# Half-height matmuls in pairs, sums on GpSimd and a written-out TensorE order in a block of attention and squared-ReLU FFN

## The chip, the cores and the metric

The kernel runs on one core of a Trainium2 chip. The metric is device time in microseconds (us) of one execution, as the median of several runs. TensorE (PE in the profile, its weight loads PEld) multiplies; VectorE (DVE), ScalarE (ACT) and GpSimd (POOL) do elementwise work; SyncE (SP) issues the transfers (DMA). Matmul results go to PSUM, a small memory that GpSimd has no part in here; all else lies in SBUF.

## The reference

One sequence of 2048 tokens with 576 features, all in float32:

```python
xn = _layernorm(x, axis=-1)
return x + _A_ref(xn, A_wqkv, A_wo) + _B_ref(xn, B_w1, B_b1, B_w2, B_b2)
# A: q, k, v = xn @ wqkv, 32 heads of 18; each token attends to 8 earlier
#    tokens at distances 0, 2, ... 14; then @ wo
# B: h = xn @ w1 + b1 (4608 wide); r = max(h, 0); (r * r) @ w2 + b2
```

## The kernel before, in words

**Number format.** Every float32 operand of a matmul is split into a high part in a shorter format that TensorE reads (float32r) and a low part, the rest. A product is then three matmuls, high by high, high by low and low by high. Feature chunks are 128 rows; 576 is four chunks and 64 rows. The last 64 features stand twice in a chunk of their own: for the activations (`xe`) the high part fills 64 rows and the low part the other 64, so one matmul with the high half of W1 covers two of the three terms, and one with the low half covers the third.

**Tiling.** The tokens are four blocks (0 to 3) of 512; two blocks form a pair `s`. The first matrix of the FFN is done for both blocks of a pair at once with a fast matrix scheme (seven products for eight): `quad(s, q, fill)` makes one of 18 steps `q` of a pair, 256 of the 4608 features. Its seven products go to three PSUM tiles `X`, `Y`, `V` (`wk` in the profile), six matmuls each and, for four of them, two more for the 64 features (`extra`). ScalarE takes snapshots (`snap`) of X between products, VectorE adds them (`add`), and ScalarE applies the relu. Results for the first block of the pair stay in SBUF (`r1`), those for the second go to HBM and come back later (`r2`, then `rs`). The scheme needs four sums of W1's parts per step; `split_w1` forms them and splits W1 into halves one step ahead.

**Squares and second matrix.** `squares` makes the high and low halves `hh`, `hl` of the squared relu; `ffn2` multiplies them with W2 into five PSUM tiles `y0` to `y4`, 28 matmuls a step (14 for each of two W2 tiles), half of it in each `fill` of the next quad. `ffn2_close` does the last step of a block chunk by chunk, and `drain` adds the residual and stores each chunk.

**Stages.** An opening part computes layernorm and q, k, v of blocks 0 and 1 (to about 116 us of the span). Then `phase_a(0)` (18 quads, with the second matrix of block 0), `phase_b(0)` from about 447 us (second matrix of block 1; layernorm and q, k, v of blocks 2 and 3), `phase_a(1)` from about 662 us, `phase_b(1)` from about 994 us. Attention (`attend`) runs on VectorE and is dealt out in small pieces: two meters count planned TensorE and VectorE time, and pieces are handed out until VectorE has 0.93 of TensorE's count. The output projection (`project`, six steps for each block) goes into the same `y` tiles.

**What sets the order.** Apart from the opening part, a scheduler places the instructions of each engine with a simulated timeline, at compile time; each engine then runs its own list in order. Tile pools fix how many buffers a tag has (`r` has 5, `w2s` 3, `w1` 4, `snap` 3), and a new tile waits until the old one in its place is done. All transfers are issued by SP, in order.

The helper `Meter` (line 60) issues all VectorE and TensorE work, so that those rows carry L60; ScalarE's copies carry L138, snapshots L507, relus L514 and L534, squares L476 and L477.

Of the kernel before, what the change touches and what calls it, by code (L numbers as in the profile page):

```python
# [9 lines left out]
F32 = mybir.dt.float32  # L10
# [33 lines left out]
LAG = 2  # L44
BEHIND = 6000.0
# [20 lines left out]
def block_kernel(ctx: ExitStack, tc: tile.TileContext, x, xt, wqkv, wo, w1, b1, w2, b2, out):  # L66
# [80 lines left out]
    def open_x(b):  # L147
        s, t = divmod(b, 2)
        xh[b] = mt.tile([P, NC - 1, TB], F32R, name="xh", bufs=2)
        xl[b] = mt.tile([P, NC - 1, TB], F32R, name="xl", bufs=2)  # L150
        if t == 0:
            xe[s] = mt.tile([P, 3, TB], F32R, name="xe")
# [43 lines left out]
    def split_e(out, v):  # L196
        nc.scalar.activation(out[:64], v[:64], AF.Copy)
        h = mt.tile([P, TB], F32R, name="he", tag="snap", bufs=3)
        nc.scalar.activation(h[64:], v[64:], AF.Copy)
        rest(out[64:], v[64:], h[64:])  # L200
# [12 lines left out]
    def halve_x(b):  # L213
        open_x(b)
        s, t = divmod(b, 2)
        for i in (0, 2):
            v = x32[b][:, i:i + 2]
            copy_hi(xh[b][:, i:i + 2], v)
            rest(xl[b][:, i:i + 2], v, xh[b][:, i:i + 2])
            yield True  # L220
        split_e(xe[s][:, t], x32e[b])
        yield True
# [8 lines left out]
    def combine_x(s):  # L231
        a, b = x32[2 * s], x32[2 * s + 1]
        sub(x32e[2 * s], x32e[2 * s], x32e[2 * s + 1])
        split_e(xe[s][:, 2], x32e[2 * s])
# [192 lines left out]
    def split_w1(n):  # L427
# [16 lines left out]
    def split_w2(n):  # L444
        if n in w2s:
            return
        r = raw2.pop(n)
        w2s[n] = mt.tile([P, 2 * D], F32R, name="w2s", bufs=3)
        split_out(w2s[n], r)
        if n < NF:  # L450
            nc.sync.dma_start(w2d[n], w2s[n].bitcast(F32))
# [21 lines left out]
    def squares(key, r):  # L473
        hh = mt.tile([P, 2, TB], F32R, name="hh", bufs=2)
        hl = mt.tile([P, 2, TB], F32R, name="hl", bufs=2)
        nc.scalar.activation(hh, r, AF.Square)  # L476
        nc.scalar.activation(r, r, AF.Square)  # L477
        rest(hl, r, hh)
        hs[key] = hh, hl

    def quad(s, q, fill):
# [9 lines left out]

        def product(p, i, first, extra=None):
# [5 lines left out]
            if extra is not None:  # L498
                f, t = extra
                w = slice(3 * K2 + f * P, 3 * K2 + (f + 1) * P)  # L500
                mm += [(hi[:, w], xe[s][:, t]), (lo[:, w], xe[s][:, t])]
            for j, (l, r) in enumerate(mm):
                ten.matmul(p, l, r, start=first and j == 0, stop=j == len(mm) - 1, skip_group_check=True)

        def snap(p, f):
            t = mt.tile([P, TB], F32, name="snap", tag="snap", bufs=3)
            nc.scalar.activation(t, p, AF.Identity, bias=bias[f])  # L507
            return t

# [9 lines left out]
        p1 = snap(X, 0)  # L519
        Y = pw.tile([P, TB], F32, name="wk")  # L520
# [12 lines left out]
        product(X, 3, False, (0, 1))  # L533
        nc.scalar.activation(r2[:, 0], X, AF.Relu, bias=bias[0])  # L534
        nc.sync.dma_start(rscr[s, q], r2)
        product(V, 4, False, (1, 2))
        add(r1[:, 1], V, u2)
        relu(r1[:, 1])
        fill(1)
        squares((b0, q), r1)  # L540

    def ffn2(b, q, parts=(0, 1)):
        if q == 0 and 0 in parts:
            yp[b] = open_y()
        hh, hl = hs[b, q]
        for i in parts:
            f = 2 * q + i
            accumulate(b, hh[:, i], hl[:, i], w2s.pop((b * NF + f)), f == 0, False)

    def load_residual(b):  # L550
        xr[b] = [pair_tile("xr") for _ in range(2)] + [mt.tile([P, TB], F32, name="xrr", tag="snap", bufs=3)]
# [290 lines left out]
    def phase_a(s):  # L842
# [3 lines left out]
        side = []  # L846
        for q in range(NQ):
            tick()
            n = s * NQ + q
            if q + 2 < NQ:  # L850
# [3 lines left out]
            if q + 1 < NQ:  # L854
                split_w1(n + 1)
            if more and q == 6:
# [5 lines left out]
            if more and q == NQ - 1:  # L862
                load_xt(b + 3)

            def fill(i, job=job):
                tick()
                job(i)
                work(side, 9.0 if q == NQ - 2 else SHARE)
                attend()

            quad(s, q, fill)
# [4 lines left out]
            attend()  # L876
            job = lambda i, q=q: ffn2(b, q, (i,))
        load_residual(b)
        assert oproj[b] == NC + 1, oproj
        return lambda: ffn2_close(b, (4, 0, 1, 2, 3))  # L880
# [19 lines left out]
    def phase_b(s, close):  # L900
        b = 2 * s + 1
        more = s + 1 < NS
        load_r(s, 0)
        job = close
        if more:
            drain_gen(halve_x(b + 1))
            side = [chain(scale_x(b + 2), halve_x(b + 2), combine_x(s + 1))]
            spare[:] = [("th", 4, 2), ("tl", 4, 2)]
            drain_gen(load_wq(0))
            rows_of = all_qkv(b + 1)  # L910
        for q in range(NQ):
# [9 lines left out]
            if more:  # L921
# [5 lines left out]
                if q >= NQ - 3 and q < NQ - 1:  # L927
                    load_w1((s + 1) * NQ + q - NQ + 3)
# [5 lines left out]
            if q == NQ - 2:  # L934
                load_residual(b)
# [52 lines left out]
```

## Time and profile before

| | |
|---|---|
| median of 3 runs | 1145.26 us (1143.19 to 1146.14) |
| the profiled execution | 1144.84 us, its span 1143.1 us |
| TensorE busy | 1120.7 us, 5003 matmuls |
| VectorE busy | 854.8 us |
| ScalarE busy | 522.3 us |
| GpSimd busy | 17.1 us |
| mean granted TensorE clock | 0.994 |
| DMA | 259.85 MB, mean 227 GB/s |

In a row of the grouped views stand the line, the engine, the operation, what is written and read, the shapes, the count, then busy us, mean ns of one, and idle time of the engine before them with what ended it. A row of the timeline or of the chain begins with its start and its length in us. A row of waits names who waited for whom, the sum in us, how often, and the longest. A row of the windows names a stretch, then its length and the busy time of TensorE, its weight loads, VectorE, ScalarE and GpSimd, the granted clock, the share of DMA and GB/s.

### The profile page before, as it was taken

What the parts mean: (1) busy time and instruction counts of PE and PEld (TensorE: products, weight loads), DVE (VectorE), ACT (ScalarE), POOL (GpSimd) and SP (SyncE); (2) the same over time, 40 slices, a digit from 0 to 9 for tenths busy, and PEclk for the clock granted to TensorE, in tenths of its full rate; (3) what the DMA queues carried; (4) which work ended last, traced back from release to release, by engine and by line L of the source; (5) the groups of instructions that cost most, each with busy time, mean ns of one, the idle gap of its engine ahead of it and who ended that gap; (6) DMA issues with size and microseconds to landing.
All of it is one profiled execution on the core that took longest, in us unless ns stands there. A gap on an engine that the chain in (4) does not pass through costs nothing.

```text
span 1143.1 us, 13647 instructions
## 1 busy us (share of the span) xinstructions
PE 1120.7 (98%) x5003; PEld 941.5 (82%) x5003; DVE 854.8 (75%) x1267; ACT 522.3 (46%) x730; POOL 17.1 (2%) x36
## 2 busy tenths in 40 slices
PE   8999999999999999999999999999999999999998
PEld 5899788878888887888888888888888888778886
DVE  6636989899889979998789878998998434263444
ACT  5343646556555455443222434535444535453452
POOL 3000000010000000000000000000000000000000
PEclk9999999999999999999999999999999999999999
DMA  7437584686584886987988966666563342575562
GB/s 246 154 107 271 219 310 152 244 288 250 198 290 173 328 308 242 347 286 270 287 294 305 351 240 213 236 238 209 216 222 133 126 155 91 193 235 195 198 191 83
DMA packets 90163, 259.85 MB, mean 227 GB/s; under 512 B 10608, under 2 KB 33776, under 8 KB 85616
## 3 DMA queue, kind: packets, MB, share of 16 engines
q1 hardware_dynamic: 89872, 258.61, 64.8%
q8 instruction: 39, 0.64, 0.2%
q10 hardware_dynamic: 224, 0.37, 0.1%
q14 instruction: 28, 0.23, 0.1%
HBM read 192.21 MB, written 66.74 MB: 227 GB/s over the span
## 4 chain that ended last, share of the span: by engine, by line
PE 85%; DMA 7%; DVE 6%; issue 1%; SPq 1%; ACT 1%; DVEq 0%; ACTq 0%
PE wk L60 44%; PE y L60 41%; DMA xb<-in_x 2%; DMA w2s<-w2d 2%; DMA wqr<-in_wqkv 1%; DMA raw<-in_w 1%; DVE xraw L60 1%; DVE pr L60 1%; DVE st L60 1%; DVE w1l L60 1%; DVE r L60 0%; DMA ob<-o 0%; DVE lg L60 0%; DVE wql L60 0%; DVE xl L60 0%
## 5 line engine op out<-in xcount | busy, mean ns | idle before, releaser
L60 PE MATMUL y<-hh,w2s 128*128 128x512 f32 x1296 | 330.2, 393 | 5.1 <-DVE xr L60 2.4
L60 PEld LDWEIGHTS y<-hh,w2s 128*128 128x128 f32 x1296 | 245.1, 190 | 58.1 <-DVE xr L60 2.8
L60 PE MATMUL y<-hl,w2s 128*128 128x512 f32 x720 | 194.4, 392 | 2.7 <-DVE hl L60 2.7
L60 PEld LDWEIGHTS y<-hl,w2s 128*128 128x128 f32 x720 | 136.3, 189 | 31.7 <-DVE hl L60 3.2
L60 DVE TENSOR_TENSOR r<-wk,snap 128x512 f32<-128x512 f32 x108 | 74.1, 686 | 94.5 <-PE wk L60 66.0
L507 ACT ACTIVATE snap<-wk,b1t 128x512 f32<-128x512 f32 x108 | 73.1, 683 | 121.1 <-PE wk L60 119.7
L60 PE MATMUL wk<-th,w1h 128*128 128x512 f32 x288 | 111.9, 390 | 0.7 <-DVE r L60 0.7
L60 PE MATMUL wk<-th,w1l 128*128 128x512 f32 x288 | 112.2, 389 | 0.0
L60 PE MATMUL wk<-tl,w1h 128*128 128x512 f32 x288 | 112.1, 389 | 0.0
L60 DVE TENSOR_TENSOR w2s<-raw,w2s 128x512 fp32r<-128x512 f32 (+1 forms) x144 | 59.3, 453 | 69.4 <-ACT w2s L138 69.4
L60 PE MATMUL wk<-wqh,xh 128*128 128x432 f32 x256 | 91.6, 365 | 2.5 <-ACT xh L138 1.1
L60 DVE TENSOR_TENSOR pr<-q,k 128x1152 f32<-128x1152 f32 x64 | 86.7, 1355 | 8.6 <-DMA k<-kscr 7.4
L60 PE MATMUL wk<-wqh,xl 128*128 128x432 f32 x256 | 91.5, 363 | 1.0 <-DVE xl L60 1.0
L60 PE MATMUL wk<-wql,xh 128*128 128x432 f32 x256 | 90.8, 361 | 1.0 <-DVE wql L60 1.0
L138 ACT ACTIVATE w1h<-raw 128x1024 fp32r<-128x1024 f32 x72 | 72.5, 1052 | 40.7 <-PE wk L60 36.1
L514 ACT ACTIVATE r<-r 128x512 f32<-128x512 f32 x108 | 67.5, 625 | 48.7 <-DVE r L60 48.6
L60 DVE TENSOR_TENSOR w1l<-raw,w1h 128x1024 fp32r<-128x1024 f32 x72 | 86.1, 1218 | 4.9 <-ACT w1h L138 4.8
L60 DVE TENSOR_TENSOR pr<-lg,v 128x1152 f32<-128x1152 f32 x64 | 86.7, 1354 | 1.2
L60 DVE TENSOR_REDUCE lg<-pr 128x64 f32<-128x1152 f32 x64 | 86.4, 1350 | 0.9
L60 PE MATMUL wk<-xh,w1h 128*128 128x512 f32 x216 | 83.5, 390 | 1.1 <-ACT snap L507 1.1
L60 PE MATMUL wk<-xl,w1h 128*128 128x512 f32 x216 | 84.1, 390 | 0.0
L60 PE MATMUL wk<-xh,w1l 128*128 128x512 f32 x216 | 84.1, 389 | 0.0
(104 smaller groups left out, 1568.4 us busy)
## 6 DMA issues: line engine op xcount, KB each, us to landing
w2s<-w2d SPq DMA_DIRECT2D x72, 576.0 KB
raw<-in_w SPq DMA_DIRECT2D x36, 640.0 KB
k<-kscr SPq DMA_DIRECT2D x16, 1296.0 KB
v<-vscr SPq DMA_DIRECT2D x16, 1296.0 KB
raw<-in_w SPq DMA_DIRECT2D x72, 288.0 KB
w2d<-w2s SPq DMA_DIRECT2D x36, 576.0 KB
r<-r SPq DMA_DIRECT2D x36, 512.0 KB
rs<-r SPq DMA_DIRECT2D x36, 512.0 KB
```

Source lines behind the costliest of these rows:

```text
L60: return f(*args, **kw)
L138: return nc.scalar.activation(out, a, AF.Copy)
L507: nc.scalar.activation(t, p, AF.Identity, bias=bias[f])
L514: nc.scalar.activation(o, o, AF.Relu)
```

## The change

Five edits come together. (1) The high half of the 64 extra features stays in its product; the low half is taken out, done with 64 rows only, and two of these stand next to each other (`low_rows`). For this the high part of the second block's `xe` lies in the upper 64 rows (`split_e`). The term low by low of these 64 features is thereby dropped. (2) The four sums of `split_w1` go from VectorE to GpSimd. (3) From `phase_a(0)` on, TensorE's order is the one in which the program is written (`manual_schedule`); the squares of a quad are placed behind the first snapshot of the next one (`early`). (4) At changes of stage: the last quad of `phase_a` squares each half on its own, starts the next x and the first q, k, v weights, and loads the residual into other tiles; the last step of a block does its first half whole; the five chunks are closed and opened in the order 4, 0, 1, 2, 3. (5) Some loads come earlier (W1 in `phase_b`, `rs`) or use other tiles (W2 of block 3 in the tag `w1`).

```diff
-        vec.tensor_tensor(out=s1, in0=a21, in1=a22, op=ALU.add)
-        sub(s2, s1, a11)
-        sub(s3, a11, a21)
-        sub(s4, a12, s2)
+        for o, u, v, op in ((s1, a21, a22, ALU.add), (s2, s1, a11, ALU.subtract),
+                            (s4, a12, s2, ALU.subtract), (s3, a11, a21, ALU.subtract)):
+            nc.gpsimd.tensor_tensor(out=o, in0=u, in1=v, op=op)
...
-                mm += [(hi[:, w], xe[s][:, t]), (lo[:, w], xe[s][:, t])]
-            for j, (l, r) in enumerate(mm):
-                ten.matmul(p, l, r, start=first and j == 0, stop=j == len(mm) - 1, skip_group_check=True)
+                mm.append((hi[:, 3 * K2 + f * P:3 * K2 + (f + 1) * P], xe[s][:, t]))
+            chain_of(p, mm, first, extra is None)
+
+        def low_rows(*three):
+            for p, f, t in three:
+                r = slice(64, P) if t == 1 else slice(0, 64)
+                chain_of(p, [(lo[r, 3 * K2 + f * P:3 * K2 + (f + 1) * P], xe[s][r, t])])
...
         p1 = snap(X, 0)
+        with tc.issue_after(taken[-1].ins):
+            early()
         Y = pw.tile([P, TB], F32, name="wk")
         product(Y, 2, True, (0, 0))
         product(X, 6, False)
         u2 = snap(X, 1)
-        add(r1[:, 0], Y, p1)
         V = pw.tile([P, TB], F32, name="wk")
         product(V, 7, True, (1, 1))
+        low_rows((Y, 0, 0), (V, 1, 1))
+        add(r1[:, 0], Y, p1)
         relu(r1[:, 0])
+        if q == NQ - 1:
+            squares((b0, q), r1, 0)
         product(X, 5, False)
         u4 = snap(X, 1)
         add(r2[:, 1], V, u4)
         fill(0)
         relu(r2[:, 1])
         product(X, 3, False, (0, 1))
+        product(V, 4, False, (1, 2))
+        low_rows((X, 0, 1), (V, 1, 2))
+        add(r1[:, 1], V, u2)
         nc.scalar.activation(r2[:, 0], X, AF.Relu, bias=bias[0])
         nc.sync.dma_start(rscr[s, q], r2)
-        product(V, 4, False, (1, 2))
-        add(r1[:, 1], V, u2)
         relu(r1[:, 1])
+        if q == NQ - 1:
+            squares((b0, q), r1, 1)
         fill(1)
-        squares((b0, q), r1)
+        return lambda: squares((b0, q), r1)
...
-    def ffn2_close(b, chunks):
-        q = NQ - 1
-        hh, hl = hs[b, q]
+    def ffn2_close(b, chunks, whole=False):
+        f = 2 * NQ - 2
+        hh, hl = hs[b, NQ - 1]
+        if whole:
+            accumulate(b, hh[:, 0], hl[:, 0], w2s[b * NF + f], False, False)
         for c in chunks:
-            for i in range(2):
-                accumulate(b, hh[:, i], hl[:, i], w2s[b * NF + 2 * q + i], False, i == 1, c)
+            for i in range(whole, 2):
+                accumulate(b, hh[:, i], hl[:, i], w2s[b * NF + f + i], False, i == 1, c)
             drain(b, c)
...
+                if ending and i == 0:
+                    if more:
+                        halves = halve_x(b + 2)
+                        next(halves)
+                        next(halves)
+                        spare[:] = [("th", 4, 2), ("tl", 4, 2)]
+                        group = load_wq(0)
+                        next(group)
+                        ahead.append(chain(halves, group))
+                    load_residual(b, (("th", 4), ("tl", 4)))
...
-    for s in range(NS):
-        close = phase_a(s)
-        phase_b(s, close)
-    ffn2_close(NB - 1, (4, 0, 1, 2, 3))
-    held.pop().close()
+    with tc.manual_schedule(engines={ET.PE}):
+        for s in range(NS):
+            phase_a(s)
+            phase_b(s)
+        ffn2_close(NB - 1, ORDER)
+        held.pop().close()
```

The change moves instructions in three places that matter below. The first is TensorE's list in the second quad of `phase_a(0)`, at its last two products. `wk` are the PSUM tiles, `w1h` and `w1l` the halves of W1; a row with `xe` and `w1l` is a low half of the 64 features. Before:

```order
L60 MATMUL wk_1267<-xe_245,w1h_1145 128x512
L60 MATMUL wk_1267<-xe_245,w1l_1146 128x512
L60 MATMUL wk_1294<-th_929,w1h_1145 128x512
L60 MATMUL wk_1294<-tl_930,w1h_1145 128x512
L60 MATMUL wk_1294<-th_929,w1l_1146 128x512
L60 MATMUL wk_1294<-th_929,w1h_1145 128x512
L60 MATMUL wk_1294<-tl_930,w1h_1145 128x512
L60 MATMUL wk_1294<-th_929,w1l_1146 128x512
L60 MATMUL wk_1294<-xe_245,w1h_1145 128x512
L60 MATMUL wk_1294<-xe_245,w1l_1146 128x512
```

Now:

```order
L61 MATMUL wk_1267<-xe_245,w1h_1147 128x512
L61 MATMUL wk_1297<-th_929,w1h_1147 128x512
L61 MATMUL wk_1297<-tl_930,w1h_1147 128x512
L61 MATMUL wk_1297<-th_929,w1l_1148 128x512
L61 MATMUL wk_1297<-th_929,w1h_1147 128x512
L61 MATMUL wk_1297<-tl_930,w1h_1147 128x512
L61 MATMUL wk_1297<-th_929,w1l_1148 128x512
L61 MATMUL wk_1297<-xe_245,w1h_1147 128x512
L61 MATMUL wk_1267<-xe_245,w1l_1148 128x512
L61 MATMUL wk_1297<-xe_245,w1l_1148 128x512
```

The low half of the first product has moved behind the second product, next to the other one; both now read 64 rows.

The second place is TensorE's list where `phase_a(1)` ends and block 2 is closed. `hl_8111` and `hh_8132` are squares of the last quad but one, `hh_8216` those of the last quad. Before:

```order
L60 MATMUL wk_8148<-xe_3938,w1l_8004 128x512
L60 MATMUL y0_5950<-hl_8111,w2s_8001 128x512
L60 MATMUL y1_5951<-hl_8111,w2s_8001 128x512
L60 MATMUL y2_5952<-hl_8111,w2s_8001 128x512
L60 MATMUL y3_5953<-hl_8111,w2s_8001 128x512
L60 MATMUL y4_5954<-hl_8111,w2s_8001 128x512
L60 MATMUL y4_5954<-hh_8216,w2s_8115 128x512
L60 MATMUL y0_5950<-hh_8216,w2s_8115 128x512 x2
```

Now:

```order
L61 MATMUL wk_8123<-xe_3977,w1l_8004 128x512
L61 MATMUL wk_8153<-xe_3977,w1l_8004 128x512
L61 MATMUL y0_6023<-hh_8132,w2s_8001 128x512
L61 MATMUL y1_6024<-hh_8132,w2s_8001 128x512
L61 MATMUL y2_6025<-hh_8132,w2s_8001 128x512
L61 MATMUL y3_6026<-hh_8132,w2s_8001 128x512
L61 MATMUL y4_6027<-hh_8132,w2s_8001 128x512
L61 MATMUL y0_6023<-hh_8132,w2s_8001 128x512
L61 MATMUL y1_6024<-hh_8132,w2s_8001 128x512
```

Before, five matmuls stand between the last product and the first use of the last quad's squares. Now a whole half step of the quad before (14 matmuls) comes first, then the first half of the last quad (14), and its second half only after these 28.

The third place is ScalarE's list at the end of `phase_a(0)`. `wqh` is the high half of the first q, k, v weights of the next block, `r_3786` before and `r_3839` now the last quad's `r1`, `rs` the same of block 1. Before:

```order
L534 ACTIVATE r_3787<-wk,b1t 128x512
L514 ACTIVATE r_3787<-r_3787 128x512
L199 ACTIVATE he<-xre 64x512
L138 ACTIVATE wqh<-wqr 128x432 x2
L197 ACTIVATE xe<-xre 64x512
L514 ACTIVATE r_3786<-r_3786 128x512
L138 ACTIVATE wqh<-wqr 128x432 x2
L476 ACTIVATE hh<-r_3786 128x1024
L138 ACTIVATE wqh<-wqr 128x432
L477 ACTIVATE r_3786<-r_3786 128x1024
L476 ACTIVATE hh<-rs 128x1024
```

Now:

```order
L139 ACTIVATE wqh<-wqr 128x432 x2
L486 ACTIVATE r_3839<-r_3839 128x512
L139 ACTIVATE w2s<-raw_3835 128x576
L139 ACTIVATE wqh<-wqr 128x432 x3
L560 ACTIVATE r_3840<-wk,b1t 128x512
L203 ACTIVATE xe<-xre 64x512
L532 ACTIVATE r_3839<-r_3839 128x512
L485 ACTIVATE hh<-rs 128x1024
L485 ACTIVATE hh<-r_3839 128x512
L486 ACTIVATE rs<-rs 128x1024
L486 ACTIVATE r_3839<-r_3839 128x512
```

The copies of `wqh` have moved ahead of the last relus, and the squares of the last quad are two halves, the second behind a square of block 1.

More of the change, by code (lines that the diff above doesn't have):

```diff
@@ L44 @@
 LAG = 2
+ORDER = (4, 0, 1, 2, 3)
 BEHIND = 6000.0
@@ L490, in quad, with chain_of @@
         bias = [b1t[:, f:f + 1] for f in (2 * q, 2 * q + 1)]
+        def chain_of(p, mm, first=False, last=True):
+            for j, (l, r) in enumerate(mm):
+                ten.matmul(p, l, r, start=first and j == 0, stop=last and j == len(mm) - 1, skip_group_check=True)
         def product(p, i, first, extra=None):
@@ L846, in phase_a @@
         side = []
+        last = lambda: None
         for q in range(NQ):
```

99 lines of the change are left out of this document (55 added, 44 removed).

## The prediction

> **What bounds the kernel now.** I read the page first, then the chain of waits, then what TensorE waited for, and last the stretches in which its clock fell.
>
> ```profile
> span 1143.1 us, 13647 instructions
> PE 1120.7 (98%) x5003; PEld 941.5 (82%) x5003; DVE 854.8 (75%) x1267; ACT 522.3 (46%) x730; POOL 17.1 (2%) x36
> PE 85%; DMA 7%; DVE 6%; issue 1%; SPq 1%; ACT 1%; DVEq 0%; ACTq 0%
> 574.06 9.54 PE y L60 x42
> 1037.43 97.78 PE y L60 x430
> ```
>
> TensorE is busy 98% of the span, and the chain runs through it for 85%. Two pieces of the chain give the pitch of a 512-wide matmul: 9.54 / 42 and 97.78 / 430, both 0.227 us. A busy TensorE says little, but a gapless row at one pitch says that only fewer or overlapping matmuls, or smaller gaps, move the end. The gaps behind the opening part (from 116 us on), and three windows around the largest:
>
> ```profile
> PE y L60 <- DVE hl L60: 2.7, 1, 2.7
> PE y L60 <- DVE xr L60: 2.4, 1, 2.4
> PE y L60 <- ACT hh L476: 1.8, 1, 1.8
> PE wk L60 <- ACT snap L507: 1.1, 2, 0.8
> PE y L60 <- DMA w2s<-w2d: 0.9, 2, 0.6
> PE wk L60 <- DVE r L60: 0.7, 1, 0.7
> ...
> 447.00:455.00 8.00, 5.28 (x17) 3.87 (x16) 7.09 (x10) 3.57 (x5) 0.00 (x0) 0.79 0.48 162
> 990.00:1001.00 11.00, 9.17 (x34) 7.10 (x33) 3.97 (x6) 5.68 (x7) 0.00 (x0) 0.84 0.77 256
> 1006.00:1015.00 9.00, 6.61 (x23) 4.92 (x22) 5.84 (x10) 2.95 (x5) 0.00 (x0) 0.81 0.82 266
> ```
>
> All waits there sum to 9.6 us, and 6.9 of them are three waits at changes of stage. In the windows the column behind the five engines is the granted clock: 0.79, 0.84 and 0.81, so each of these waits also costs (1 - 0.79) x 8 = 1.7, 1.8 and 1.7 us of slow matmuls. The changes of stage cost 6.9 + 5.2 = 12.1 us in all; the rest of the time is matmuls.
>
> The profiled execution took 1144.84 us, span and 1.74 us around it; the median of the runs is 1145.26, so the sum below can stand for both.
>
> **Half-height pairs.** Removed are 144 full matmuls with the low half of the last 64 features; added are 144 of 64 rows, in 72 pairs whose two members lie in different halves of the array and go to different PSUM tiles.
>
> ```profile
> L60 PE MATMUL wk<-xe,w1l x144: 388/389/398, 110.7 to 992.9; 128*128 128x512 f32 x144
> ```
>
> No row shows two matmuls at once, so the price of a pair is bounded. Below: both stream together and a pair costs one pitch, 0.227. Above: nothing overlaps (0.454), and each change of height also lays bare the tail of the matmul before, duration less pitch, 0.389 - 0.227 = 0.162, twice: 0.778. Between lies what the start behind a stall shows:
>
> ```profile
> 117.72 0.50 PE L60 MATMUL wk<-xh,w1h 128*128 128x512 f32 x1 [0.78 <-ACT snap L507]
> 117.83 0.19 PEld L60 LDWEIGHTS wk<-xl,w1h 128*128 128x128 f32 x1
> 118.06 0.40 PE L60 MATMUL wk<-xl,w1h 128*128 128x512 f32 x1
> ```
>
> The second matmul starts 0.34 behind the first instead of 0.227: a weight load that could not run ahead costs 0.11. Inside a stream it never shows, since weights load under the matmul in front. A pair's second weights go to the other half of the array, so I take them as hidden too, the row of the gapless stream being the nearest: 0.227 a pair. That saves 72 x (0.454 - 0.227) = 16.4 us; the ends are 16.4 saved and 72 x (0.778 - 0.454) = 23.3 lost.
>
> The Trainium skill speaks on both sides. "TensorE: Matmul & The Clock Gate", Part 3, has matmuls in different row groups start about 4 ns apart, by which the estimate of a pair would be 0.231 us and the saving 16.1. "TensorEngine Tiling (Array Packing)", Key Properties, says that a change of tiling mode drains the TensorE; that is the second rival below. No row of this kernel shows either.
>
> **Block 2 to 3 (TensorE's last change of stage).** Two waits go, 1.8 and 2.4 us, with their slow clock, 1.8 and 1.7.
>
> ```profile
> 1008.68 0.71 DVE L60 STREAM_TRANSPOSE ot<-ob 128x512 f32<-128x512 f32 x1 [3.92 <-DMA ob<-o]
> 1009.31 0.71 DVE L60 SCALAR_TENSOR_TENSOR xr<-y,b2t,xr 128x512 f32<-128x512 f32 x1
> ...
> L60 DVE TENSOR_TENSOR r<-wk,snap 128x512 f32<-128x512 f32 x108 | 74.1, 686 | 94.5 <-PE wk L60 66.0 <-ACT snap L507 27.9
> L514 ACT ACTIVATE r<-r 128x512 f32<-128x512 f32 x108 | 67.5, 625 | 48.7 <-DVE r L60 48.6
> L476 ACT ACTIVATE hh<-rs 128x1024 fp32r<-128x1024 f32 x36 | 38.1, 1060 | 96.0 <-PE y L60 73.0 <-DMA rs<-r 22.9
> ```
>
> The 2.4 were a drain of y queued on VectorE behind a transpose that sat 3.92 us for a gather. In the new order the drains stand ahead of the transposes. The 1.8 were the last quad's squares, needed 5 matmuls behind its last product. Now 28 matmuls stand between that product and the second half's first use: 28 x 0.227 = 6.4 us. The work to be hidden is an addition (0.69), a relu (0.63), a half square (bounded by the equally wide relu, 0.63), the other block's square (1.06), the second half square (0.63) and a subtraction (0.69): 4.3. It fits. I leave 0.3 for the last drain of chunk 4, which has a split of W2 in front of it: 7.7 - 0.3 = 7.4 saved. If the cover were gone, the 1.8 and its clock would be back.
>
> **Block 0 to 1.** Here 2.7 + 1.7 = 4.4 us are lost now, for the same squares.
>
> ```profile
> L138 ACT ACTIVATE w2s<-raw 128x576 fp32r<-128x576 f32 x72 | 49.0, 683 | 65.1 <-PE y L60 49.1 <-DMA raw<-in_w 10.6 <-PE wk L60 4.1
> L138 ACT ACTIVATE wqh<-wqr 128x432 fp32r<-128x432 f32 x35 | 17.5, 554 | 17.0 <-DMA wqr<-in_wqkv 10.3 <-PE wk L60 6.7
> 435.17 6.50 DMA wqr<-in_wqkv
> ```
>
> The cover is again 6.4 us. Behind the last product ScalarE has two relus, a copy of xe and two half squares (0.69 + 0.63 + 0.62 + 2 x 0.63) and the other block's two squares (2 x 1.06): 5.3, with the subtraction 6.0. But in front of them stand four copies of fresh weights (0.68 + 3 x 0.55 = 2.3) that wait for a transfer of 6.5 us, issued only when product 5 is done. If they are on time nothing is left of the wait; if they are late by their full length, 6.0 + 2.3 - 6.4 = 2, and up to 2.9 with a late landing. I take 1.7, under the 1.8 at which the clock fell above: 2.7 saved. In that last quad two 1.05 us copies of the next x stand ahead of the second snapshot; about 1 us is added for it.
>
> **Sums on GpSimd.** VectorE loses 144 additions, GpSimd gains them.
>
> ```profile
> L60 DVE TENSOR_TENSOR raw<-raw 128x256 f32<-128x256 f32 x144 | 56.6, 418 | 9.4 <-DMA raw<-in_w 9.1
> L60 DVE TENSOR_TENSOR wql<-wqr,wqh 128x432 fp32r<-128x432 f32 x35 | 19.7, 600 | 9.4 <-ACT wqh L138 9.2 <-DMA q<-q 0.3
> 9.78 2.04 DVE L671 TENSOR_TENSOR wql<-wq,wqh 128x432 fp32r<-128x432 f32 x2
> 9.82 1.54 POOL L671 TENSOR_TENSOR wql<-wq,wqh 128x432 fp32r<-128x432 f32 x1 [0.32 <-ACT wqh L138]
> 11.87 1.11 POOL L671 TENSOR_TENSOR wql<-wq,wqh 128x432 fp32r<-128x432 f32 x1
> 116.00:447.00 331.00, 329.16 (x1455) 272.57 (x1454) 295.94 (x485) 182.56 (x258) 5.83 (x8) 1.00 0.70 252
> 662.00:866.00 204.00, 204.00 (x902) 168.99 (x901) 182.25 (x253) 91.67 (x125) 0.00 (x0) 1.00 0.60 211
> ```
>
> GpSimd needs 1.11 us for 432 columns alone, so for 256 between 0.66 (in proportion) and 1.11 (all fixed); I take 0.8. Four in a row are 3.2 us of a quad's 17, a quad ahead of their use, so their latency is hidden. But the two engines hinder each other: side by side, GpSimd's 1.11 became 1.54, and two subtractions on VectorE took 2.04 instead of 2 x 0.60. VectorE idles 35.1 us over the 18 quads up to 447 and 21.8 over the 11 up to 866, 1.95 a quad; what the sums free is filled again, since attention is paced by counted TensorE time. A quad is also shorter by two pitches, so 1.5 us a quad may be lost to the hindrance before anyone waits. Between no cost and the fourth rival below, I take 2 us for the whole kernel.
>
> **Edits at nothing.** TensorE in traced order waits if a result is late, with nothing to fill in. In a quad, the second snapshot stands behind a square pair (2.1 us) that starts with the first; it ends 13 matmuls and 0.9 us behind product 1, and product 5 comes 8 pitches behind the 13: 0.9 us to spare. Residuals, W1 and x load earlier or in other tiles on the same queue; the stages in which they move keep the transfers they had. Each microsecond of that cover that fails costs 36 us over the quads.
>
> **Sum.** 1144.84 - 16.4 (pairs) - 7.4 - 2.7 (changes of stage) + 1 (last quads) + 2 (GpSimd) = 1121.3, say **1122 us**.
>
> **Rivals.** First, the second weights of a pair load only when its first matmul has started: 0.11 more a pair, 72 x 0.11 = 7.9, **1129 us**. For it: a load begins right behind the start of a matmul in the rows above, never earlier. Against it: the other half of the array is free.
>
> Second, each change of height drains the array: 2 x 0.162 x 72 = 23.3 more, **1145 us**, no change at all. For it: a duration is 0.162 longer than the pitch, so there is a tail to drain; against it, nothing in this trace changes height. The Trainium skill's rule on tiling modes, named above, is this case.
>
> Third, the change does not do what it says: the halves run one behind the other at 0.227 each, 16.4 more, **1138 us**. Against it: they share neither rows nor PSUM.
>
> Fourth, the other side: the port. If every one of the four sums stops VectorE for 0.66 us, it loses 2.6 a quad with 1.5 to spare, and each of the 29 quads with attention grows by 1.1: 33 us, **1154 us**. It decides from 0.38 us a sum on. For it: the pair of rows at 9.8. Against it: much of VectorE's work is reductions and additions from PSUM, under which a sum can run.
>
> **How the numbers follow.** Chances: forecast 0.45, exposed weights 0.20, no overlap 0.10, drains 0.14, port 0.11. The forecast's own range is 1115 to 1127. The range 1114 to 1146 takes in the first three rivals and leaves out the port and what is worse than the drains alone. A measurement of this kernel tells 0.3%, 3.4 us, from no change. Forecast, exposed weights and no overlap are faster: 0.75. Of the drains 0.09 lie within 0.3% and 0.05 beyond it; with the port, slower is 0.16.
>
> **What would show it.** Pairs: start to start of the two half-height matmuls near zero, and the next full one a pitch later; 0.11 or 0.39 instead names the rival. Stages: no wait on hl, hh or xr above 1.8 us behind block 2, a granted clock of 1.00 there, one of at most 2.9 behind block 0. GpSimd: sums of 0.7 to 1.1 us and no growing waits of TensorE on r or snap; such waits in the quads of both first stages would make the forecast wrong from above.

## The result, and the profile after

The changed kernel takes 1154.30 us (median of 7 runs, 1151.40 to 1156.54), the kernel before on the same chip 1145.52 (7 runs, 1143.19 to 1148.58). The ratio is 1.0074, with a 95% interval of 1.0056 to 1.0093: slower by 8.8 us, where 1122 was forecast. The profiled execution took 1155.61 us. First the page, then the group of the half-height matmuls among the rows by form (least, median and greatest duration in ns, first and last start):

```profile
span 1153.9 us, 13722 instructions
PE 1132.8 (98%) x5003; PEld 921.3 (80%) x5003; DVE 834.4 (72%) x1125; ACT 524.0 (45%) x734; POOL 167.6 (15%) x180
```
```profile
L61 PE MATMUL wk<-xe,w1l x144: 491/495/499, 112.4 to 1008.7; 64*128 64x512 f32 x144
```

TensorE still fills 98% of a span that is 10.8 us longer; 144 half-height matmuls last 0.495 us each where the full ones lasted 0.389. The timeline shows what stands around one pair; first TensorE, then its weight loads:

```profile
207.57 0.39 PE L61 MATMUL wk<-xe,w1h 128*128 128x512 f32 x1
207.89 0.50 PE L61 MATMUL wk<-xe,w1l 64*128 64x512 f32 x2
208.32 0.96 PE L61 MATMUL y<-hh,w2s 128*128 128x512 f32 x3
```
```profile
207.12 0.19 PEld L61 LDWEIGHTS wk<-th,w1l 128*128 128x128 f32 x1
207.35 0.19 PEld L61 LDWEIGHTS wk<-xe,w1h 128*128 128x128 f32 x1
207.89 0.19 PEld L61 LDWEIGHTS wk<-xe,w1l 64*128 64x128 f32 x2 [0.35 <-issue]
208.32 0.76 PEld L61 LDWEIGHTS y<-hh,w2s 128*128 128x128 f32 x4 [0.24 <-issue]
```

The two halves do run at once: both lie in one row of 0.50 us. But each change of height costs on both sides. A full matmul's weights load a pitch ahead of it (207.35 for the one at 207.57). The weights of the first half load only at 207.89, with the matmul itself, 0.32 us behind the start of the full matmul before instead of 0.227. The next full matmul and its weights come 0.43 behind the halves, where the forecast had one pitch. Over all 72 pairs the medians from start to start are 0.318 (full to half), 0.003 (half to half), 0.4245 (half to full) and 0.338 (that full one to the next): 1.084 us against 0.908 for four pitches, 0.18 a pair more than the two full matmuls that were there. Each change of height has two parts in these starts. The first, 0.318 - 0.227 = 0.09, is read here as a drain of the array. The second is a weight load that could not run ahead, 0.11 as behind a stall: that of the half lies in the 0.4245 (0.227 + 0.11 + a second drain of 0.09), that of the next full matmul in the 0.338 (0.227 + 0.11). Together 2 x (0.09 + 0.11) = 0.40 us a pair.

The waits of TensorE behind the opening part, and the windows around them (columns as before):

```profile
PE y L61 <- DMA w2s<-w2d: 5.2, 2, 3.0
PE y L61 <- DVE hl L61: 2.5, 2, 1.4
PE y L61 <- ACT hh L485: 0.9, 1, 0.9
PE y L61 <- ACT w2s L139: 0.2, 1, 0.2
PE wk L61 <- ACT snap L523: 0.2, 1, 0.2
```
```profile
445.00:455.00 10.00, 8.90 (x42) 7.50 (x41) 10.00 (x16) 6.48 (x10) 0.00 (x0) 1.00 0.88 348
562.00:574.00 12.00, 8.99 (x28) 7.04 (x27) 9.53 (x11) 3.40 (x6) 0.00 (x0) 0.72 0.74 271
663.00:673.00 10.00, 7.85 (x28) 5.97 (x27) 9.90 (x8) 0.11 (x1) 3.20 (x3) 0.83 0.80 309
1017.00:1026.00 9.00, 8.09 (x36) 6.39 (x35) 5.92 (x9) 2.54 (x3) 0.00 (x0) 1.00 0.66 182
```

At the changes of stage (about 447 and 1019 us) the waits are down to 1.1 and 0.9 + 0.2 us and the granted clock is 1.00: the 12.1 us there fell to 2.2. In their place stand two waits for `w2s` inside `phase_b(0)`, 3.0 and 2.15 us, with clocks of 0.72 and 0.83 behind them: (1 - 0.72) x 12 = 3.4 and (1 - 0.83) x 10 = 1.7 us more, 10.3 in all, where the kernel before waited 0.9 us for `w2s`. Another 1.4 us for `hl` stand at the first step of the second matrix.

So by the trace: pairs 72 x 0.18 = +13, waits for `w2s` 10.3 - 0.9 = +9.4, the first `hl` +1.4, changes of stage -9.9, a shorter opening part and small waits about -2 (the first row with `xe` and `w1h` begins at 108.9 us instead of 110.4, and the waits for `snap` and `r` behind it are 0.8 us less): about +12, against 10.8 measured.

GpSimd's new work, and the VectorE rows that it meets:

```profile
L446 POOL TENSOR_TENSOR raw<-raw 128x256 f32<-128x256 f32 x144 | 150.9, 1068 | 731.9 <-DMA raw<-in_w 575.7
L61 DVE TENSOR_TENSOR w1l<-raw,w1h 128x1024 fp32r<-128x1024 f32 x72 | 89.3, 1263 | 9.3 <-ACT w1h L139 9.3
```

VectorE gave up 56.6 us of sums, and its busy time fell by only 20.4 (854.8 to 834.4). By this difference 36 us, 0.25 a sum, went into slower rows of its own (this one from 1.22 to 1.26 us). The rows that both kernels have in equal form and number are 25 us longer by their own durations, 0.17 a sum, so the loss lies between the two. Waits for `r` or `snap` did not grow.

### The profile page after: what moved, and what is told of

Read it like the earlier page. It is cut to its first block, busy times and chain, and to the rows that moved or that the text cites. A ratio compares the mean times of both kernels' runs of the same rounds, so it can differ in the third digit from the quotient of the medians.

```text
span 1153.9 us, 13722 instructions
## 1 busy us (share of the span) xinstructions
PE 1132.8 (98%) x5003; PEld 921.3 (80%) x5003; DVE 834.4 (72%) x1125; ACT 524.0 (45%) x734; POOL 167.6 (15%) x180
## 4 chain that ended last, share of the span: by engine, by line
PE 89%; DMA 6%; DVE 3%; ACT 1%; issue 1%; SPq 1%; POOL 0%; DVEq 0%; POOLq 0%
PE wk L61 46%; PE y L61 42%; DMA wqr<-in_wqkv 2%; DMA w2s<-w2d 1%; DMA raw<-in_w 1%; DVE xraw L61 1%; DMA q<-qkv 1%; DMA xb<-in_x 1%; DVE hl L61 0%; DVE xr L61 0%; DVE pr L61 0%; DVE wql L61 0%; DMA vscr<-qkv 0%; DVE w2s L61 0%; DVE st L61 0%
## 5 line engine op out<-in xcount | busy, mean ns | idle before, releaser
L61 PE MATMUL y<-hh,w2s 128*128 128x512 f32 x1296 | 334.5, 396 | 6.3 <-DMA w2s<-w2d 5.2
L61 PEld LDWEIGHTS y<-hh,w2s 128*128 128x128 f32 x1296 | 242.6, 189 | 65.3 <-issue 8.3
L446 POOL TENSOR_TENSOR raw<-raw 128x256 f32<-128x256 f32 x144 | 150.9, 1068 | 731.9 <-DMA raw<-in_w 575.7
L61 PE MATMUL y<-hl,w2s 128*128 128x512 f32 x720 | 197.8, 393 | 2.5 <-DVE hl L61 2.5
L61 PE MATMUL wk<-th,w1h 128*128 128x512 f32 x288 | 116.3, 404 | 0.2 <-ACT snap L523 0.2
L61 DVE TENSOR_TENSOR w1l<-raw,w1h 128x1024 fp32r<-128x1024 f32 x72 | 89.3, 1263 | 9.3 <-ACT w1h L139 9.3
L61 DVE TENSOR_TENSOR pr<-lg,v 128x1152 f32<-128x1152 f32 x64 | 89.4, 1397 | 1.6
L61 DVE TENSOR_TENSOR hl<-r,hh 128x1024 fp32r<-128x1024 f32 (+1 forms) x38 | 45.9, 1209 | 56.0 <-ACT r L486 55.7
L61 DVE TENSOR_TENSOR pr<-pr 128x576 f32<-128x576 f32 (+1 forms) x128 | 84.4, 660 | 2.1
```

The lines of the kernel that those rows point to most:

```text
L61: return f(*args, **kw)
L446: nc.gpsimd.tensor_tensor(out=o, in0=u, in1=v, op=op)
```

## The experiments

Theory: the pairs lose 12 us by their changes of height, the traced order loses some 5 to 10 us in `phase_b(0)`, and the changes of stage gain 10. Rivals: the pairs gain as forecast and all is lost in the order; or GpSimd and VectorE hold each other up and TensorE pays. The ratios are against the kernel before, run on the same chip each time. Where two versions are set side by side, the text subtracts their medians, and adds what the ratios give where that differs by more than 1 us.

**full_low: no change of height.**

```diff
-                r = slice(64, P) if t == 1 else slice(0, 64)
+                r = slice(None)
```

> The changed kernel with one word different: the low half of the last chunk is multiplied by full-height matmuls (128 rows) in the places where the pairs of half height stood, so no change of height is left; every engine's order of instructions is that of the changed kernel. (The term is then low half by high part plus low half by rest; the changed kernel leaves the second out.) Theory T, from the trace of the changed kernel: a pair takes 0.625 us of TensorE's time where two full matmuls take 0.454, so 72 pairs give back 12.3 us: 1154 - 12.3 = 1142 us. Rival A, the forecast's price: a pair costs one pitch of 0.227 us and what was lost was lost elsewhere; then the full matmuls cost 16.4 us more: 1154 + 16.4 = 1170 us. Rival B, half the halves' price is hidden by work that waits anyway: within 2 us of 1154.

Measured: 1142.66 us (10 runs), ratio 0.9972 (0.9954 to 0.9990), 11.6 us below the changed kernel. Theory T. The third stage holds the same matmuls in both kernels, apart from the pairs' heights, and no long wait; its first and last row with `xe` and `w1h` give its length. For this kernel, then for the changed one:

```profile
L61 PE MATMUL wk<-xe,w1h x72: 389/389/389, 670.0 to 996.4; 128*128 128x512 f32 x72
```
```profile
L61 PE MATMUL wk<-xe,w1h x72: 388/389/390, 675.0 to 1008.4; 128*128 128x512 f32 x72
```

326.4 against 333.4 us with 35 pairs between: 7.0 / 35 = 0.20 us a pair, where the starts gave 0.18. So 72 pairs are 13 to 14 us. The whole gained 11.6, since two other things differ: the first wait for `snap` ends at 118.5 us here and at 115.3 in the changed kernel, 3.2 later, and the second of the two waits for `w2s` is 1.7 us with a clock of 1.00, some 2 us less.

**twice and one_half: what in a pair costs.** The first issues each pair twice in a row, by a second loop in `low_rows`:

```diff
             for p, f, t in three:
                 r = slice(64, P) if t == 1 else slice(0, 64)
                 chain_of(p, [(lo[r, 3 * K2 + f * P:3 * K2 + (f + 1) * P], xe[s][r, t])])
+            for p, f, t in three:
+                r = slice(64, P) if t == 1 else slice(0, 64)
+                chain_of(p, [(lo[r, 3 * K2 + f * P:3 * K2 + (f + 1) * P], xe[s][r, t])])
```

The second issues only the first member:

```diff
-            for p, f, t in three:
+            for p, f, t in three[:1]:
```

Expected of twice:

> The changed kernel with each pair of half-height matmuls issued twice in a row (the low term is counted twice, so the output is not the reference's): four halves between the same two changes of height. Theory T, the price hangs on the change of height, and halves of equal height run two at a time: the second pair adds one pitch of 0.227 us, or 0.34 us where its weights are not hidden under the first pair: 72 x 0.227 = 16 us to 72 x 0.34 = 24.5 us, so 1170 to 1179 us. Rival H, each pair pays the whole 0.625 us that a pair now costs: 72 x 0.625 = 45 us, 1199 us.

Expected of one_half:

> The changed kernel with only the first half-height matmul of each pair (the low terms of V are left out, so the output is not the reference's): 72 matmuls fewer, the changes of height stay. Theory T, a pair's price is the change of height and its second member rides along free: from the full matmul before a half to the second full one behind it stay 1.08 us, as with a pair, and the time stays near that of the changed kernel, 1150 to 1158 us (the plan of the other engines shifts a little with it). Rival W, the second member's weight load is part of the price: 0.11 less each, 1.08 becomes 0.97 and the time falls by 8 us to 1146. Rival X, the second member costs its own pitch: 0.227 less each, 0.85 us and 16 us, 1138 us.

Measured: twice 1174.87 us (ratio 1.0272, 1.0234 to 1.0310), 20.6 above the changed kernel, within T's range. one_half 1149.57 (1.0043, 1.0020 to 1.0065), 0.4 below T's range, so the trace has to decide. The third stage of both, twice first:

```profile
L61 PE MATMUL wk<-xe,w1h x72: 388/388/393, 683.1 to 1025.2; 128*128 128x512 f32 x72
```
```profile
L61 PE MATMUL wk<-xe,w1h x72: 387/389/390, 668.7 to 1002.2; 128*128 128x512 f32 x72
```

With one half the stage lasts 333.5 us, with a pair 333.4: the second member is free, and leaving it out buys nothing. With two pairs it lasts 342.1, 8.7 / 35 = 0.25 a pair, about one pitch. The timelines around one place say the same, again twice first:

```profile
211.49 0.39 PE L61 MATMUL wk<-xe,w1h 128*128 128x512 f32 x1
211.81 0.73 PE L61 MATMUL wk<-xe,w1l 64*128 64x512 f32 x4
212.47 1.20 PE L61 MATMUL y<-hh,w2s 128*128 128x512 f32 x4
```
```profile
209.22 0.39 PE L61 MATMUL wk<-xe,w1h 128*128 128x512 f32 x1
209.54 0.49 PE L61 MATMUL wk<-xe,w1l 64*128 64x512 f32 x1
209.96 2.37 PE L61 MATMUL y<-hh,w2s 128*128 128x512 f32 x9
```

From the full matmul to the next full one pass 0.98 us with two pairs, 0.74 with one half, 0.75 with a pair. So going to half height and back costs about 0.65 - 0.25 = 0.4 us whatever is done there, and each pair 0.25 on top where two full matmuls cost 0.454. By this estimate two pairs at one change of height are about even and three are the first to gain; three were not run. By its trace, what one_half saved against the changed kernel came in `phase_b(0)`, where its plan left one wait for `w2s` of 1.6 us without a slow clock instead of two with one.

**sched_b0: TensorE's order in `phase_b(0)` back to the scheduler.**

```diff
-    with tc.manual_schedule(engines={ET.PE}):
-        for s in range(NS):
-            phase_a(s)
-            phase_b(s)
+    traced = {ET.PE}
+    with tc.manual_schedule(engines=traced):
+        phase_a(0)
+    phase_b(0)
+    with tc.manual_schedule(engines=traced):
+        phase_a(1)
+        phase_b(1)
```

> The changed kernel with TensorE's order in the second phase (second block's second half of the feed-forward net beside the next rows' q, k and v; 447 to 670 us) left to the scheduler, as before the change; the other phases keep the traced order. Theory T: the two waits for w2s at 563 us (3.0 us, and 3.4 us more by half clock) and at 665 us (2.15 us, and 1.7 us more) come from the traced order, which has nothing else to give TensorE when w2s is late; they go, or fall under 1 us in all, and the time is 8 to 11 us lower: 1143 to 1146 us. Rival S: w2s is late because of what stands ahead of it in SP's queue (the moved loads), whatever TensorE's order; waits of 3 to 5 us remain and the time is 1150 to 1155 us.

Measured: 1149.50 us (6 runs, 1.0045, 1.0026 to 1.0064): 4.8 below the changed kernel (3.3 by the ratios), half of what T said or less, and 0.5 below the range that S allowed. Its waits in the trace, and the window around the one for `w2s`, fit T for the most part:

```profile
PE y L61 <- DVE xrr L61: 1.5, 1, 1.5
PE y L61 <- DMA w2s<-w2d: 1.4, 1, 1.4
PE y L61 <- DVE hl L61: 1.4, 1, 1.4
```
```profile
558.00:570.00 12.00, 10.58 (x53) 9.44 (x52) 6.69 (x9) 4.72 (x7) 0.00 (x0) 1.00 1.02 344
```

One wait for `w2s` is left, and no slow clock. SP's queue shows why the first load is late. In the changed kernel SP issues the two `w2s` at 560.35, behind a load of q, k, v weights and three stores:

```profile
557.92 0.33 SPq L373 DMA_DIRECT2D o<-q  x1
558.36 0.37 SPq L276 DMA_DIRECT2D wqr<-in_wqkv  x1
558.82 0.41 SPq L296 DMA_DIRECT2D q<-qkv  x1
559.27 0.44 SPq L296 DMA_DIRECT2D kscr<-qkv  x1
559.76 0.49 SPq L296 DMA_DIRECT2D vscr<-qkv  x1
560.35 0.99 SPq L430 DMA_DIRECT2D w2s<-w2d  x2
```

TensorE is through with the work ahead at 563.7 and restarts at 566.68. In sched_b0 SP issues them at 560.37, no earlier; there TensorE has other matmuls first. So this load is late in both, and the traced order sets what that costs: S was right on the lateness, T on the price. That the loads moved in the queue make it late is read from these rows and was not tried.

At 665 us the changed kernel runs y matmuls alone and idles; sched_b0 places W1 work of the next stage between them and never stops. Here the queue is not what delays the load. By the chain it is issued at 658.91, right behind the row of y matmuls that ends at 658.90, and takes 8.43 us, where the median of these loads is 4.4:

```profile
655.69 3.21 PE y L61 x14
658.91 8.43 DMA w2s<-w2d
```

**vec_sums: the sums back on VectorE,** not counted in the pacing of attention, TensorE's order unchanged.

```diff
-            nc.gpsimd.tensor_tensor(out=o, in0=u, in1=v, op=op)
+            nc.vector.tensor_tensor(out=o, in0=u, in1=v, op=op)
```

> The changed kernel with the four sums of a W1 quad back on VectorE instead of GpSimd; TensorE's order is that of the changed kernel, word for word. Theory T: the slow GpSimd sums (1068 ns mean, 151 us in all) and the slowed VectorE instructions stand under TensorE's work, TensorE hardly ever waits for r or snap in either kernel, so the time stays within 2 us of 1154. Rival P (the two engines hold each other up and TensorE pays): the span falls by 5 to 10 us, 1144 to 1149. Rival V (VectorE is short of time): it rises by several us, since 144 instructions of some 0.4 to 0.5 us (about 65 us) come back to VectorE.

Measured: 1160.77 us (4 runs, 1.0136, 1.0115 to 1.0156), 6.5 above the changed kernel. Theory T fell; it is rival V, and P is out in this form. The wait for `hl` at 446 us is 3.6 us instead of 1.1: VectorE is late at the change of stage.

```profile
PE y L61 <- DVE hl L61: 3.6, 1, 3.6
```

The sums are uncounted on both sides here, so this is a step of the engine alone, and GpSimd is the better by 6.5 us.

**full_sched: full height, and the scheduler's order in `phase_b(0)`:** the edits of full_low and sched_b0 together.

> The changed kernel with both edits at once: full-height matmuls in place of the pairs, and TensorE's order in the second phase (447 to 670 us) left to the scheduler. Theory T (pairs and traced order in the second phase are two separate losses, one by one 11.6 us and 4.8 us at the median): they add, 1154.3 - 11.6 - 4.8 = 1138 us, 1136 to 1140, faster than both kernels. Rival O: the scheduler's gain is used up elsewhere once the first phase is shorter (14 matmuls that it leaves for the third phase, waits behind the last change of stage): 1141 to 1144 us, no better than with the full matmuls alone.

Measured: 1137.63 us (12 runs), ratio 0.9942 (0.9921 to 0.9962). Theory T: the two losses add, and this version beats both kernels, by 7.4 us (before) and 16.7 (changed). Against full_low the scheduler's order in `phase_b(0)` is worth 5.0 us (3.4 by the ratios). Its longest waits:

```profile
PE wk L61 <- ACT snap L523: 2.4, 3, 1.5
PE y L61 <- DMA w2s<-w2d: 1.7, 1, 1.7
PE y L61 <- DVE hl L61: 1.6, 1, 1.6
```

No wait is above 1.7 us, and the granted clock is 1.00 around each of those behind 440 us.

**full_free: full_low without any traced order.**

```diff
-    with tc.manual_schedule(engines={ET.PE}):
+    if True:
```

> The changed kernel with full-height matmuls and no traced order at all: the scheduler sets TensorE's order in all phases, as before the change. Theory T: outside the second phase the traced order is worth nothing either way, so within 2 us of full_sched (1136 to 1140 us). Rival Q: the traced order keeps each quad's chains and the closing at the changes of stage in their places; without it the waits for snap, hl and xr come back and the time is 1141 to 1147 us.

Measured: 1144.44 us (10 runs, 1.0001, 0.9982 to 1.0021), 6.8 above full_sched: rival Q by the time, though the waits are not those that Q named (`snap`, `hl`, `xr`). The traced order earns in the other stages what it loses in `phase_b(0)`, and a little more: with it everywhere (full_low) the time is 1142.66 us. Without it:

```profile
PE wk L61 <- DVE r L61: 5.3, 6, 1.4
PE y L61 <- ACT w2s L139: 3.9, 1, 3.9
```

**The sums, with and without the rest.** before_gp is the kernel before with the sums on GpSimd; before_gp_paced the same with the sums counted as if VectorE still did them. full_sched_vec is full_sched with the sums on VectorE, counted; full_sched_paced is full_sched with the sums on GpSimd, counted. full_free_vec is full_free with the sums on VectorE: only the changes of stage and the moved loads are left of the change.

```diff
-        vec.tensor_tensor(out=s1, in0=a21, in1=a22, op=ALU.add)
-        sub(s2, s1, a11)
-        sub(s3, a11, a21)
-        sub(s4, a12, s2)
+        for o, u, v, op in ((s1, a21, a22, ALU.add), (s2, s1, a11, ALU.subtract),
+                            (s4, a12, s2, ALU.subtract), (s3, a11, a21, ALU.subtract)):
+            nc.gpsimd.tensor_tensor(out=o, in0=u, in1=v, op=op)
```

In the two paced kernels one line more stands ahead of the sum; full_sched_vec and full_free_vec have `vec.tensor_tensor` in its place:

```diff
+            vec.spent += vec.fixed + vec.each * K2
             nc.gpsimd.tensor_tensor(out=o, in0=u, in1=v, op=op)
...
-            nc.gpsimd.tensor_tensor(out=o, in0=u, in1=v, op=op)
+            vec.tensor_tensor(out=o, in0=u, in1=v, op=op)
```

Expected of full_sched_vec:

> full_sched with the four sums of a W1 quad on VectorE and counted in the pacing of the attention work, as before the change. Theory G (the sums on GpSimd relieve VectorE where it is late, at the changes of stage): 4 to 6 us slower than full_sched, with longer waits of TensorE on hl, xrr or snap behind 440 and 990 us. Theory N (what the sums on VectorE cost when they were tried alone, 6.5 us, came from their not being counted in the pacing): within 2 us of full_sched. Theory P (GpSimd and VectorE hold each other up): 3 us or more faster than full_sched.

Expected of before_gp:

> The kernel before with one edit of the change, the four sums of a W1 quad on GpSimd (order s4 before s3 as in the change). Theory G: VectorE is done earlier at the changes of stage, so the waits for hl at 447 us (2.7 us, 1.7 more by half clock) and for xr at 1007 us (2.4 and 1.7) shrink: 3 to 6 us faster, 1140 to 1143 us. Theory N: 1144 to 1148 us. Theory P: slower by 2 us (the forecast's term) to 10 us: 1148 to 1156 us.

Expected of before_gp_paced:

> The kernel before with the four sums on GpSimd, as in the run that had only this edit and took 8.8 us more, but with the sums counted in the pacing of the attention work as if VectorE still did them, so that attention work is dealt out as before. Theory N2 (the loss came from more attention work being dealt to VectorE, since the sums no longer counted): it goes, 1143 to 1148 us. Theory P2 (the two engines hold each other up, and what TensorE then waits for at the changes of stage is late whatever the pacing): 1151 to 1156 us. In between, 1148 to 1151 us, both have a part.

Expected of full_sched_paced:

> full_sched (1137.6 us) with the sums on GpSimd counted in the pacing as if VectorE did them. Theory N2: the stages' new order already takes the waits away, so pacing hardly matters: 1135 to 1139 us, within 2 us of full_sched. Rival: attention work dealt out later leaves VectorE late behind 990 us or makes waits on wos, as where the sums were on VectorE: 1139 to 1143 us.

Expected of full_free_vec:

> The changed kernel without three of its edits: full-height matmuls, no traced order, W1's sums on VectorE and counted in the pacing. What is left of the change is the other order at the changes of stage and the moved loads. The forecast's price for these is 10.1 us: 1145 - 10 = 1135 us, 1133 to 1138. Rival R: part of what they gained beside the GpSimd sums (1153.8 to 1144.4 us) was only what the sums had lost there; alone they are worth 0 to 4 us, 1141 to 1145 us.

| | sums on VectorE, counted | on GpSimd, counted | on GpSimd, not counted |
|---|---|---|---|
| kernel before | 1 (1145 us) | before_gp_paced 1.0015 (0.9995 to 1.0036), 1147.86 us | before_gp 1.0074 (1.0056 to 1.0092), 1153.84 us |
| full_sched | full_sched_vec 0.9945 (0.9925 to 0.9966), 1138.74 us | full_sched_paced 0.9980 (0.9962 to 0.9999), 1143.71 us | full_sched 0.9942 (0.9921 to 0.9962), 1137.63 us |
| full_free | full_free_vec 0.9973 (0.9958 to 0.9989), 1142.92 us | | full_free 1.0001 (0.9982 to 1.0021), 1144.44 us |

The first step to the right is the engine alone: by the ratios 0.15% in the kernel before, which is within the measurement, and 0.35% in full_sched, about 2 and 4 us (by the medians 2.8 and 5.0), both against GpSimd. The second step is the dealing out of attention alone, and it has no sign of its own: 6.0 us lost in the kernel before, 6.1 gained in full_sched (6.8 and 4.4 by the ratios). Nor has the engine one: in vec_sums, uncounted, GpSimd was the better by 6.5.

So theory G fell in both of its tests; only in vec_sums, with the sums uncounted on VectorE, did GpSimd's share show as relief (a wait for `hl` of 1.1 us instead of 3.6). N holds for full_sched_vec (1.1 us from full_sched) and not for before_gp, whose time lies in P's range. The cause is for the most part not P's: counting the sums takes 6.0 of the 8.8 us away again, as N2 said (1147.86, at the edge of its 1143 to 1148). For full_sched_paced it is the rival, 0.7 us above its range. In before_gp the uncounted sums let more attention be dealt to VectorE, and TensorE waits longer for VectorE at the old changes of stage (6.4 and 3.8 us, where it was 2.7 and 2.4):

```profile
PE y L60 <- DVE hl L60: 6.4, 3, 4.7
PE y L60 <- DVE xr L60: 3.8, 1, 3.8
```

The trace of before_gp_paced bears this out for `hl` only; it is of one of its slower runs (1151.35 us), and what the median run waits for is not shown:

```profile
PE wk L60 <- DVE r L60: 5.9, 2, 4.2
PE y L60 <- DVE xr L60: 4.6, 1, 4.6
PE y L60 <- DVE hl L60: 2.8, 2, 2.0
```

full_sched_paced waits for `wos` instead, 3.0 us in one piece. Why its dealing suits the new order worse is not settled: full_sched_vec has the same count and nearly the same waits for `wos`.

full_free_vec answers for the changes of stage and the moved loads alone: 0.9973, 3 us, where the forecast priced them at 10.1 together. Rival R, but not for R's reason only. The wait at 447 us is gone, and new waits have come: 4.0 us for `r`, most of it in the quads of `phase_a(0)`, and 3.9 for `w2s` behind block 2, with a clock of 0.81 there:

```profile
PE wk L61 <- DVE r L61: 4.0, 4, 1.8
PE y L61 <- ACT w2s L139: 3.9, 1, 3.9
```
```profile
1015.00:1024.00 9.00, 5.10 (x17) 3.80 (x16) 7.30 (x13) 4.60 (x6) 0.00 (x0) 0.81 0.94 322
```

With the traced order outside `phase_b(0)` they shrink to 0.2 and 0.3 us (full_sched_vec, 0.9945; the intervals of the two ratios touch). So the edit seems to need that order to keep what it gains.

**The way from one kernel to the other,** in medians: 1145.0 before; sums on GpSimd 1153.8; changes of stage and loads 1144.4; traced order outside `phase_b(0)` 1137.6; traced order inside it 1142.7; pairs 1154.3. Taken in another order the middle steps come out differently, as the table shows; the last one is the same kernel with one line changed.

## Why the prediction was wrong

**Bound.** Right: TensorE's row of matmuls sets the end, and what the traces account for is matmul intervals, waits of TensorE and slow clocks behind them.

**Half-height pairs.** This is the step that failed. The lower bound, one pitch a pair and 16.4 us saved, was taken; measured is a loss of 11.6 us (0.18 to 0.20 a pair by the traces), a difference of 28 us out of the 32 by which 1122 was missed. The overlap that the forecast chose was there: the members start 3 ns apart. The Trainium skill's "TensorE: Matmul & The Clock Gate", Part 3, has about 4 ns, and the trace agrees. The second weights, about which the forecast asked, cost nothing (one_half). What was wrong is that it put the change of height at nothing: a pair was to take "one pitch", with the weights hidden, "the row of the gapless stream being the nearest". That row holds for equal heights only. The nearest row was the one quoted a few lines above, the start behind a stall, where a load that could not run ahead cost 0.11: each change of height is such a start, after a drain of 0.09, on both sides, 0.40 us a pair.

The second rival named half of the mechanism, the drain. The Trainium skill, "TensorEngine Tiling (Array Packing)", Key Properties, names it too: changing the tiling mode drains TensorE. The traces agree, with 0.09 us each way. The rival's price, 2 x 0.162 = 0.324 a pair, put the drains too high and left out the two weight loads behind them (2 x 0.11): 0.55 a pair by its sum, 0.63 to 0.65 measured. That is still inside the upper bound of 0.778. The first rival (second weights exposed, 0.11) and the third (no overlap) are out: halves 3 ns apart.

**Changes of stage.** In the trace of the changed kernel right to within 1 us: 7.4 forecast, 6.6 found (7.7 less 0.9 and 0.2) behind block 2; 2.7 forecast, 3.3 found (4.4 less 1.1) behind block 0. Alone, with the moved loads, the edit is worth 3 us: without the traced order other waits take the place.

**Last quads, +1.** Found 0.2 (`snap`).

**GpSimd, +2.** With the sums counted, the engine alone costs 2 to 4 us, near the term; with them uncounted, as the change has them, it gained 6.5 in the changed kernel (vec_sums). So that the term's size was met in one case is luck in part. The mean duration was within what was forecast (1.07, where 0.7 to 1.1 was said; single sums took 0.73 to 1.95). The fourth rival needed 0.38 us a sum; VectorE lost 0.17 to 0.25. What the term left out is that the sums no longer count in the pacing: 6 us either way.

**Edits at nothing.** In sum nearly right, by two errors that cancel: with full-height matmuls the traced order loses 5.0 us in `phase_b(0)` and gains 6.8 outside it, 1.8 gained in all. The forecast looked for the traced order's risk in the quads, where its 0.9 us of cover held. It said nothing of `phase_b(0)`, where the traced order takes away the work that covered late `w2s` loads, and it asked only whether the stages keep their transfers, not what then stands ahead of `w2s` in SP's queue. Nor did it see that the changes of stage need the traced order.

Put together along the way above, of the 32 us: +28 for the pairs, +7 for the sums (8.8 where 2 was said), the changes of stage as forecast (9.4 gained where 9.1 was said, the last quads with them), -7 for the traced order outside `phase_b(0)` and +5 inside it. Along another way the middle terms differ; that they nearly cancel is luck. The pairs at their measured price alone give 1122 + 28 = 1150, beyond the range's 1146: it stopped at the drains, without the weights behind them and without a loss elsewhere. The loads in `phase_b(0)` were in no case.

## What to carry to other kernels

Going to half height and back in a dense stream costs 0.4 us of TensorE here, and half-height pairs of 512 columns earn about 0.2 each, so by this estimate they pay only where three or more stand together. Before a fixed order replaces a scheduler's, list the places where late loads were covered by work of another stage: a stage can be fixed and its neighbour left free, and that was the fastest version here (1137.6 us, full_sched_vec within the measurement of it). Moving work off an engine that paces other work changes the pacing too; count it both ways before pricing the move.

## What the runs showed of the hardware that was not expected

Leaving out one matmul of a half-height pair changes no time at all (333.5 against 333.4 us for a stage with 35 of them). Whether a stall of middle length slows the clock is open until it runs: a wait of 1.8 us in the kernel before was followed by a clock of 0.84 in its window; the same wait, 1.8 us again, in before_gp_paced and one of 2.5 us in twice were followed by 1.00 throughout. The second wait and both windows, that of before_gp_paced first:

```profile
PE y L61 <- DVE xrr L61: 2.5, 1, 2.5
```
```profile
995.00:1006.00 11.00, 8.35 (x36) 6.25 (x35) 4.83 (x7) 5.68 (x7) 0.00 (x0) 1.00 0.79 259
```
```profile
1034.00:1046.00 12.00, 9.48 (x42) 7.53 (x41) 6.72 (x11) 2.69 (x3) 0.00 (x0) 1.00 0.64 174
```

The 13 single waits of 2.7 us and more in the traces of these kernels, behind the opening part, were all followed by a slow clock. So a slow clock behind a wait of about 2 us is a chance and not a term: of the 12.1 us that the changes of stage seemed to cost, 3.5 were of this kind, those behind the waits of 1.8 and 2.4.
